# Attention with a convolved feed-forward layer on one core: probabilities cast and split by units of two slots, some squares halved on GpSimd, and a new order of all steps

## The chip, the core and the metric

The kernel runs on one core of a Trainium2 chip. That core has five engines with a queue of instructions each: TensorE (PE in the profile, with PEld for its weight loads), VectorE (DVE), ScalarE (ACT), GpSimd (POOL) and SyncE (SP), which here starts the DMA transfers. The metric is the device time of one execution in microseconds (us); lower is better.

## What is computed

The reference, cut to what matters. There are 8 batches and 12 heads, 448 positions, 64 features a head; the feed-forward layer goes from 768 to 1024 and back, with a convolution over 3 neighbouring positions as its gate.

```python
def _attn_ref(q, k, v, g_q, g_k):
    def rmsnorm(x, g):
        rms = np.sqrt(np.mean(x * x, axis=-1, keepdims=True) + 1e-06)
        return x / rms * g
    q_n, k_n = (rmsnorm(q, g_q), rmsnorm(k, g_k))
    scores = 1.0 / np.sqrt(q.shape[-1]) * np.matmul(q_n, k_n.transpose(0, 1, 3, 2))
    attn = np.exp(scores - np.max(scores, axis=-1, keepdims=True))
    attn = attn / (np.sum(attn, axis=-1, keepdims=True) + 1e-09)
    return np.matmul(attn, v).astype(np.float32)

def _moe_ref(x, w_in, conv_w, w_out):
    h = np.maximum(x @ w_in, 0.0)
    ...
    for k in range(K):
        conv_out += conv_w[k][None, None, :] * hp[:, k:k + S, :]
    gate = 1.0 / (1.0 + np.exp(-conv_out))
    return (h * gate @ w_out).astype(np.float32)
```

## The kernel before, in words

**Pairs and slots.** The work of attention goes by pairs of heads, 48 in all, six to a batch. The queries of a pair, 2 x 448 rows, are cut into seven blocks of 128 rows, which the code calls slots (`SLOTS`). The slots form four units (`GROUPS`): three units of two slots, one from each head, and a unit of one slot that holds the rest of both heads.

**Float32 by halves.** Most matmuls take numbers as two float16 parts: a cast ("hi") and the remainder of the cast ("lo"). Names ending in `_hi` and `_lo` make these parts.

**The steps of a pair.** `load_k` and `load_q` bring the rows (L355, L362). `square` makes the squares on ACT or POOL, `square_sum` adds them up by groups of 64 on DVE (L382), nine `rsqrt` steps make the factors for two pairs at once (a `duo`), and `apply_rms` applies them. `qk_transpose` turns q and k on PE (L481), `qk_hi` and `qk_lo` make their parts. `scores` multiplies a unit (L656), `soft_max` takes the maxima from PSUM on DVE (L664 when the two banks are neighbours, else L669), and `soft_exp` makes the exponentials of a slot on ACT (L679) into `e`, a ring of three buffers of one slot.

**Two ways to turn the probabilities.** Up to pair 9 PE transposes them (`p_transpose`, L726, and `p_evac`). From pair 10 on (`n1=10`, and `dg=7`: all seven slots) they are turned by DMA. `p_hi` casts a slot into `ph` (at the helper's line L83). `p_lo` subtracts the cast from the exponentials in two instructions, 384 and 64 columns (at L95). `p_turn` then transposes the whole unit by one DMA on SP (L717). `pv` (L815) multiplies with v, whose parts `v_hi` and `v_lo` (L792) make. `sum_add` to `sum_load` bring the sums of the exponentials to every partition by way of DRAM, with one small transpose on PE (L746), and `x_scale` (L822), `x_hi` and `x_lo` make x.

**Feed-forward.** For each batch `in_part` (L889) multiplies x by `w_in` in eight feature groups; relu, convolution, tanh and gate follow on ACT and DVE; `in_hi` and `in_lo` make the parts, `out_part` (L968) multiplies by `w_out`, `out_evac` and `out_store` write the result. Some feature groups of the first and last batch start early (`nf`, `nl`): their first matmuls run while later pairs of the batch are not done.

**The order.** No engine chooses at run time. The program writes down a plan: `at(time, step)` gives each step a due time, in which `base(n)` for pair n is `T0` us per pair for the first five pairs and `T` after that. `needs` lists what a step waits for, with the rings of buffers (`BUFS`) among it. `options` lists the engines a step may run on, with a cost for each. A list scheduler then takes, again and again, the step that can start soonest, with due times as a weight, and so fixes the engine, the PSUM bank and the place of every step in its engine's queue. Each queue is worked off strictly in that order. The constants in `PH` are the plan's parameters.

**Shared helpers.** `copy` (L83), `copy_scaled` (L87 to L89) and `binary` (L95) issue most casts and two-source operations; so one line of the profile stands for many steps, and the names of the tiles tell them apart.

Of the kernel before, what the change touches and what calls it, by code (L numbers as in the profile page):

```python
# [10 lines left out]
F32 = mybir.dt.float32  # L11
# [8 lines left out]
PH = dict(  # L20
    T0=11.354, N0=5, T=16.716, ti=26.404, si=4.968, so=8.683, hop=0.561, beta=0.03, wi0=-36.475,
    wi1=117.871, wo0=26.473, wo1=140.589, cw=-9.559, tg=-80.912, tl=42.69, ea=0.946, te=111.903,
    ep=0, hs=0, nf=2, adj=0.197, nz=8, ne=0, sc=5, tc=2, mc=8, p_qe=0.801, p_evac=0.876,
    p_hi=1.239, p_lo=6.052, p_rms=2.091, p_v=1.03, p_x=0.071, p_g=2.256, p_relu=0.553,
    p_cv=1.183, p_qz=0.843, p_ev=6.268, sp=0.158, nbulk=6, p_rs=0.05, p_sq=0.889, p_w=0.585,
    v0=-6.625, dg=7, n1=10, sw=0.0, nl=2, tj=0.0, pvs=1, pk=0.1, p_sa=0.167, p_ph=0.417,
    p_pl=0.839, nq=3, nk=95, p_qh=0.526, p_ql=0.365, tq=10.598, ti0=0.056, ti1=0.097, ti2=-0.224,
    ti3=0.742, ti4=-0.239, ti5=-0.006, ti6=0.553, ti7=-0.022, si0=0.995, si1=1.566, si2=1.683,
    si3=1.415, si4=1.633, si5=1.199, si6=1.05, si7=1.338, to0=0.019, to1=0.173, to2=-0.044,
    to3=0.041, to4=0.226, to5=-0.307, to6=-0.084, to7=0.325, so0=1.015, so1=1.613, so2=1.833,  # L30
    so3=1.736, so4=1.784, so5=1.547, so6=1.25, so7=1.038,
# [23 lines left out]
def tile_attention_moe(ctx: ExitStack, tc, q, k, v, g_q, g_k, w_in, conv_w, w_out, out):  # L55
# [41 lines left out]
    def move(e, dst, src):  # L97
# [9 lines left out]
        qkf=3, sq=2, st=2, qT=2, kT=2, qz=2, v=8, sst=6, e=3, PT=2, x=12, c=3,  # L107
# [24 lines left out]
    def bank(tag, key):  # L132
        i = bank_of[tag, key]
        assert bank_now[i] == (tag, key), f"{tag} {key} is gone"
        return banks[:, i]

    def old(tag, key):
        return rings[tag][tag, key]
# [20 lines left out]
    ebuf = [const.tile([P, 512], F32, name=f"e{i}") for i in range(BUFS["e"])]  # L159
# [216 lines left out]

    def square_sum(n):
        m = duo(n)[0]
        w = D // 2 if n < PH["hs"] else D
        if m == n:  # L380
            new("st", n, [P, 4, duo(n)[1], 2, 2 * NB], F32)
        nc.vector.tensor_reduce(  # L382
            old("st", m)[:, 0, n - m].rearrange("p i s -> p (i s)"),
            old("sq", n).rearrange("p i h t d -> p (i h t) d")[..., :w], axis=AX.X, op=ALU.add,
        )
# [144 lines left out]
    def plan_qk(n):  # L530
# [5 lines left out]
        if n < PH["hs"]:  # L536
            at(s - 23.0, square_half, n)
# [120 lines left out]
    def soft_max(n, g):  # L658
        js = GROUPS[g]
        st, at = new("sst", (n, g), [P, 2], F32), [bank_of["s", (n, j)] for j in js]  # L660
        for j in js:
            bank("s", (n, j))
        if at[-1] == at[0] + 1:
            nc.vector.tensor_reduce(  # L664
                st, banks[:, at[0] : at[0] + 2, :S], axis=AX.X, op=ALU.max, negate=True
            )
        else:
            for u, i in enumerate(at):
                nc.vector.tensor_reduce(  # L669
                    st[:, u : u + 1], banks[:, i, :S], axis=AX.X, op=ALU.max, negate=True  # L670
                )

    def soft_exp(n, j):
        if j == 0:
            new("rsum", n, [P, NS], F32)
        c = SLOTS[j]
        ring = rings.setdefault("e", Ring(BUFS["e"]))
        e = ring.put(("e", (n, j)), ebuf[ring.count % BUFS["e"]])
        nc.scalar.activation(  # L679
            e[:, :S], bank("s", (n, j))[:, :S], AF.Exp,  # L680
            bias=old("sst", (n, unit(j)[0]))[:, unit(j)[1] : unit(j)[1] + 1],
            accum_out=old("rsum", n)[:, c : c + 1],
        )


# [4 lines left out]
    def p_hi(n, j):  # L690
        u, i, _ = unit(j)
        if i == 0:
            ring = rings.setdefault("ph", Ring(BUFS["ph"]))
            ring.put(("ph", (n, u)), phbuf[ring.count % BUFS["ph"]])
        copy(
            on["p_hi", n, j], parts(n, j)[:, :4],
            old("e", (n, j)).rearrange("p (c k) -> p c k", c=4),
        )

    def parts(n, j):  # L700

        u, i, js = unit(j)
        m = len(js)
        blocks = old("ph", (n, u))[:, : 7 * m * P]
        return blocks.rearrange("p (c i k) -> p c i k", c=7, i=m)[:, :, i]

    def p_lo(n, j):
        p, e = parts(n, j), old("e", (n, j))[:, :S]
        binary(
            on["p_lo", n, j], p[:, 4:], e[:, : 3 * P].rearrange("p (c k) -> p c k", c=3),  # L710
            p[:, :3], ALU.subtract,
        )
        binary(on["p_lo", n, j], p[:, 3, 64:], e[:, 3 * P :], p[:, 3, :64], ALU.subtract)
# [8 lines left out]
    def p_transpose(n, j):  # L722
        ps, e = new_bank("t", ("p", n, j)), old("e", (n, j))
        for kt in range(NB):
            k0 = min(kt * P, S - P)
            nc.tensor.transpose(ps[:, kt * P : (kt + 1) * P], e[:, k0 : k0 + P], ident)  # L726
# [104 lines left out]
    def plan_attention(n):  # L831
# [3 lines left out]
        for j in range(NS):  # L835
            if unit(j)[1] == 0:
                at(s + j * d + 1.0, soft_max, n, unit(j)[0])
            at(s + j * d + 2.0, soft_exp, n, j)
            if j < nd(n):
                at(s + j * d + 3.0, p_hi, n, j)  # L840
                at(s + j * d + 4.0, p_lo, n, j)
                if j == unit(j)[2][-1]:
                    at(s + j * d + 5.0, p_turn, n, unit(j)[0])
                continue
            at(s + j * d + 4.0, p_transpose, n, j)
            at(s + j * d + 5.0, p_evac, n, j)
# [189 lines left out]
    def prepare():  # L1036
# [19 lines left out]
        for z in ebuf:  # L1056
            nc.gpsimd.memset(z[:, S:], 0.0)
# [48 lines left out]
    def needs(name, *a):  # L1106
# [109 lines left out]
        elif name == "v_load":  # L1216
            yield "pv", n - BUFS["v"], pvs(n - BUFS["v"])[-1]
# [30 lines left out]
        elif name == "soft_exp":  # L1248
# [3 lines left out]
            m, j = back(n, a[1], BUFS["e"])  # L1252
            yield ("p_lo" if j < nd(m) else "p_transpose"), m, j
            yield "sum_transpose", n - BUFS["rsum"]
        elif name == "p_hi":
            yield "soft_exp", *a
            if a[1] or not nd(n - 1):
                yield "p_hi", n, a[1] - 1
            else:
                yield "p_hi", n - 1, nd(n - 1) - 1  # L1260
            m, u = back(n, unit(a[1])[0], BUFS["ph"], NG)
# [4 lines left out]
        elif name == "p_turn":  # L1266
            for j in GROUPS[a[1]]:
                yield "p_lo", n, j
# [119 lines left out]
    def joined(n, g):  # L1388

        i, j = (bank_of["s", (n, j)] for j in (GROUPS[g][0], GROUPS[g][-1]))  # L1390
        return j == i + 1

    def options(name, *a):
        wo = a and a[0] == "out"
        dma = lambda kind, c, k=1, g="C": ("ACT" if kind in ON_ACT.split() else "SP", c, (g, k))
        dve, act, pool, pe = (lambda c, e=e: (e, c, None) for e in ("DVE", "ACT", "POOL", "PE"))
        return dict(
# [21 lines left out]
            square_sum=lambda: [dve(0.67 if a[0] < PH["hs"] else 1.21)],  # L1419
# [16 lines left out]
            soft_max=lambda: [dve(1.08 if joined(*a) else 0.61 * len(GROUPS[a[1]]))],  # L1436
# [34 lines left out]
            p_hi=lambda: [act(0.61), pool(0.62), dve(0.46)],  # L1471
            p_lo=lambda: [pool(1.22), dve(0.95)],
# [259 lines left out]
```

## Time and profile before

| what | value |
|---|---|
| median of 3 runs | 883.34 us (879.39 to 883.75) |
| the profiled execution | 882.48 us |
| its span, first to last instruction | 880.7 us |
| mean granted clock of TensorE | 0.984 |
| matmuls on PE | 5416 |
| DMA transfers | 132.69 MB, mean 151 GB/s |

How to read it. The page's first part gives each engine's busy time, its share of the span and its number of instructions. The second part cuts the span into 40 slices of 22 us, with a digit for tenths of busy time; `PEclk` is the TensorE clock that was granted, in tenths of full speed. The windows view gives the same for any stretch. In the lines view a row is a group of instructions of one line, engine, operation and tiles, with busy time, mean duration, and the idle time of the engine just before them. The waits view says who waited for whom: total, number of times, longest. The timeline lists instructions in order of time, with the idle time before one in brackets and what ended it.

### The profile page before, as it was taken

How to read it: one execution, taken by the hardware profiler on the slowest of the kernel's cores; microseconds unless marked ns; L12 is line 12 of the kernel's file. 1: busy time of each engine (PE TensorE's matmuls, PEld its weight loads, DVE VectorE, ACT ScalarE, POOL GpSimd, SP SyncE). 2: the span in 40 equal slices, each digit the busy share in tenths (PEclk: the TensorE clock that was granted, in tenths of full speed). 3: DMA queues.
4: the chain of work that ended last, by engine and by line, in shares of the span. 5: the costliest groups of instructions: out<-in, count | busy, mean ns of one | idle time of the engine just before them, and what ended most of it. 6: DMA issues, size and time to landing. Idle time of an engine off the chain costs nothing.

```text
span 880.7 us, 16865 instructions
## 1 busy us (share of the span) xinstructions
PE 817.6 (93%) x5416; PEld 417.4 (47%) x5416; DVE 732.5 (83%) x1256; ACT 685.1 (78%) x1571; POOL 642.0 (73%) x968
## 2 busy tenths in 40 slices
PE   1588999999998799999999999998999999999998
PEld 0343445545543345455444454454455554555554
DVE  6999999987899998999988887999899898972330
ACT  3677889888787978888887878897798878784441
POOL 4446667868787978988878987887787887884120
PEclk9989999999999899999999999999999999999999
DMA  8875542138997778897886898877796898458001
GB/s 248 216 225 130 162 108 67 44 83 185 175 191 147 159 168 179 168 188 163 180 184 134 183 173 184 184 163 153 176 183 147 165 191 163 102 93 163 28 13 60
DMA packets 344740, 132.69 MB, mean 151 GB/s; under 512 B 304612, under 2 KB 342860, under 8 KB 343884
## 3 DMA queue, kind: packets, MB, share of 16 engines
q1 hardware_dynamic: 344652, 131.62, 68.8%
q8 instruction: 43, 0.70, 0.3%
q14 instruction: 45, 0.37, 0.2%
HBM read 58.22 MB, written 11.18 MB: 79 GB/s over the span
## 4 chain that ended last, share of the span: by engine, by line
PE 64%; DVE 16%; DMA 6%; ACT 5%; POOL 4%; issue 4%; SPq 1%; DVEq 0%; ACTq 0%; POOLq 0%
PE banks L968 20%; PE banks L889 19%; PE banks L656 9%; PE banks L815 9%; PE banks L481 4%; PE banks L806 2%; POOL ph L95 2%; ACT e L679 2%; DMA wo<-in_moe_w_in_dram 2%; DMA rB<-rd 1%; PE banks L726 1%; DMA PT<-ph 1%; DVE st L382 1%; DVE wo L232 1%; DMA qk<-in_q_dram 1%
## 5 line engine op out<-in xcount | busy, mean ns | idle before, releaser
L95 POOL TENSOR_TENSOR ph<-e,ph 128x384 f16<-128x384 f32 x468 | 291.3, 647 | 53.1 <-ACT ph L83 49.5
L889 PE MATMUL banks<-x,wi 128*128 128x448 f16 x1152 | 250.1, 354 | 1.3 <-DVE kT L517 0.5
L968 PE MATMUL banks<-wo,gring 128*128 128x384 f16 (+1 forms) x1056 | 210.9, 328 | 2.1 <-DVE kT L517 1.8
L889 PEld LDWEIGHTS <-wi 128*128 128x128 f16 x1152 | 108.7, 98 | 102.0 <-issue 17.0
L83 ACT CAST ph<-e 128x512 f16<-128x512 f32 x244 | 147.7, 614 | 9.9 <-DMA PT<-ph 7.2
L968 PEld LDWEIGHTS <-gring 128*128 128x128 f16 (+1 forms) x1056 | 100.3, 99 | 78.1 <-issue 22.3
L656 PE MATMUL banks<-kT,qT 64*128 64x448 f16 x864 | 106.4, 361 | 8.8 <-DVE qT L519 6.3
L815 PE MATMUL banks<-PT,vp 128*64 128x448 f16 (+1 forms) x836 | 97.4, 363 | 4.5 <-ACT e L679 2.7
L95 POOL TENSOR_TENSOR sq<-qk,st 128x512 f32<-128x512 f32 (+1 forms) x78 | 85.4, 1108 | 6.2 <-DVE st L404 4.1
L481 PE MATMUL banks<-ident,sq 128*128 128x128 f32 (+1 forms) x364 | 60.8, 280 | 17.5 <-POOL sq L95 16.6
L95 POOL TENSOR_TENSOR x<-rB,x 128x448 f16<-128x448 f32 x48 | 51.5, 1073 | 23.5 <-ACT x L83 20.9
L815 PEld LDWEIGHTS <-vp 128*64 128x64 f16 (+1 forms) x836 | 41.8, 109 | 54.2 <-issue 33.8
L382 DVE TENSOR_REDUCE st<-sq 128x16 f32<-128x1024 f32 x48 | 57.6, 1206 | 9.6 <-ACT sq L369 9.6
L481 PEld LDWEIGHTS banks<-ident,sq 128*128 128x128 f32 (+1 forms) x364 | 44.5, 145 | 43.7 <-POOL sq L95 18.7
L656 PEld LDWEIGHTS <-qT 64*128 64x128 f16 x864 | 34.3, 95 | 64.2 <-issue 32.2
L726 PE MATMUL banks<-ident,e 128*128 128x128 f32 x280 | 45.8, 294 | 11.2 <-ACT PT L83 6.9
L822 DVE TENSOR_TENSOR rB<-banks,rB 128x448 f32<-128x448 f32 x48 | 29.6, 617 | 29.9 <-PE banks L815 14.5
L528 POOL COPY qz<-qT 64x128 f16<-64x128 f16 x89 | 32.9, 370 | 23.7 <-DVE qT L519 15.7
L726 PEld LDWEIGHTS banks<-ident,e 128*128 128x128 f32 x280 | 32.8, 147 | 31.4 <-ACT PT L83 13.3
L968 PE MATMUL banks<-wo,wi 128*128 128x384 f16 (+1 forms) x192 | 46.9, 326 | 0.0
L83 ACT COPY PT<-banks 128x512 f32<-128x512 f32 x66 | 38.0, 584 | 10.7 <-PE banks L726 10.2
L369 ACT ACTIVATE sq<-qk 128x1024 f32<-128x1024 f32 x35 | 36.7, 1050 | 7.8 <-DMA qk<-in_q_dram 7.8
(1154 smaller groups left out, 1726.9 us busy)
## 6 DMA issues: line engine op xcount, KB each, us to landing
qk<-in_q_dram SPq DMA_DIRECT2D x48, 224.0 KB
rB<-rd SPq DMA_DIRECT2D x96, 112.0 KB
qk<-in_k_dram SPq DMA_DIRECT2D x48, 128.0 KB
wo<-in_moe_w_in_dram SPq DMA_DIRECT2D x6, 1024.0 KB
v<-in_v_dram SPq DMA_DIRECT2D x48, 128.0 KB
gring<-in_moe_w_out_dram SPq DMA_DIRECT2D x8, 768.0 KB
qk<-in_k_dram SPq DMA_DIRECT2D x48, 96.0 KB
v<-in_v_dram SPq DMA_DIRECT2D x48, 96.0 KB
```

Source lines behind the costliest of these rows:

```text
L83: (nc.scalar.copy if e == "ACT" else elementwise(e).tensor_copy)(dst, src)
L95: elementwise(e).tensor_tensor(dst, a, b, op=op)
L369: nc.scalar.activation(sq, old("qkf", n), AF.Square)
L382: nc.vector.tensor_reduce(old("st", m)[:, 0, n - m].rearrange("p i s -> p (i s)"), old("sq", n).rearrange("p i h t d -> p (i h t) d")[..., ...
L481: nc.tensor.transpose(ps[:, t * w : t * w + m], x[:m, t], ident[:m, :m])
L528: e.tensor_copy(z[HALF[h], :, HALF[h]], old("qT", n)[HALF[h], :, t0 : t0 + 64])
L656: nc.tensor.matmul(ps[u][:, :S], lhs, kt[r, w], start=(i == 0), stop=(i == 2))
L726: nc.tensor.transpose(ps[:, kt * P : (kt + 1) * P], e[:, k0 : k0 + P], ident)
L815: nc.tensor.matmul(ps[HALF[h], :S], v[:m, w, h, c % 4], pt[:m, c, h * S : (h + 1) * S], start=(i == 0), stop=(i == len(PV7) - 1),)
L822: nc.vector.tensor_tensor(t, bank("m", ("v", n))[:, :S], t, op=ALU.mult)
L889: nc.tensor.matmul(ps[:, :S], wi[:, wl, c, fc * P : (fc + 1) * P], old("x", b * NP + c)[:, xl], start=(i == 0), stop=(i == 3 * NP - 1),)
L968: nc.tensor.matmul(ps[p0 : p0 + m, :NO2], g, wo[:, wl, fc, half * NO2 : (half + 1) * NO2], start=(i == 0), stop=(i == 3 * NFC - 1),)
```

## The change

1. `e` becomes a ring of two buffers, each with room for the two slots of a unit. `soft_exp` still makes one slot at a time and waits, at the first slot of a unit, for the remainders of the unit two before.
2. `p_hi` casts a unit in one instruction, through an access pattern that reads 4 x 128 columns of each slot at a stride of 448. `p_lo` makes the remainders of a unit in two instructions, 2 x 3 x 128 and 2 x 64 columns. `p_turn` waits for the one `p_lo`.
3. `square_half` existed, but ran for no pair (`hs=0`). A new `halved(n)` is true for `n >= 10` and `n % 4 < 2` (`hk=2`): there POOL adds the second half of each group of 64 squares to the first, and `square_sum` reduces 32 columns in place of 64.
4. The ring of v has 7 buffers in place of 8, and from the eighth load on a load waits for `v_lo` of the pair seven earlier, where that pair has one, in place of `pv` of the pair eight earlier.
5. The planner's costs for the new shapes are put in, and its parameters `PH` change: among others `T0` from 11.354 to 11.0, `T` from 16.716 to 16.382, `nl` from 2 to 3 and `nk` from 95 to 94. So the order of all steps, and the engine of some, is made anew.

The core of the diff:

```diff
-    T0=11.354, N0=5, T=16.716, ti=26.404, si=4.968, so=8.683, hop=0.561, beta=0.03, wi0=-36.475,
+    T0=11.0, N0=5, T=16.382, ti=26.404, si=4.968, so=8.766, hop=0.561, beta=0.03, wi0=-36.475,
...
-    v0=-6.625, dg=7, n1=10, sw=0.0, nl=2, tj=0.0, pvs=1, pk=0.1, p_sa=0.167, p_ph=0.417,
-    p_pl=0.839, nq=3, nk=95, p_qh=0.526, p_ql=0.365, tq=10.598, ti0=0.056, ti1=0.097, ti2=-0.224,
+    v0=-6.625, dg=7, n1=10, sw=0.0, nl=3, tj=-0.038, hk=2, pvs=1, pk=0.1, p_sa=0.167, p_ph=0.417,
+    p_pl=0.748, nq=3, nk=94, p_qh=0.526, p_ql=0.384, tq=10.598, ti0=0.04, ti1=0.123, ti2=-0.224,
...
-        qkf=3, sq=2, st=2, qT=2, kT=2, qz=2, v=8, sst=6, e=3, PT=2, x=12, c=3,
+        qkf=3, sq=2, st=2, qT=2, kT=2, qz=2, v=7, sst=6, e=2, PT=2, x=12, c=3,
...
-    ebuf = [const.tile([P, 512], F32, name=f"e{i}") for i in range(BUFS["e"])]
+    ebuf = [const.tile([P, 2 * S + 64], F32, name=f"e{i}") for i in range(BUFS["e"])]
...
+    def halved(n):
+
+        return n < PH["hs"] or n >= PH["n1"] and n % 4 < PH["hk"]
...
-        w = D // 2 if n < PH["hs"] else D
+        w = D // 2 if halved(n) else D
...
-        if n < PH["hs"]:
+        if halved(n):
             at(s - 23.0, square_half, n)
...
+    def e_slot(n, j):
+
+        u, i, _ = unit(j)
+        return old("e", (n, u))[:, S * i : S * (i + 1)]
...
+    def parts(n, u):
+
+        m, e = len(GROUPS[u]), old("e", (n, u))
+        blocks = old("ph", (n, u))[:, : 7 * m * P]
+        return (
+            blocks.rearrange("p (c i k) -> p i c k", c=7, i=m),
+            bass.AP(e.tensor, e.offset, [e.ap[0], [S, m], [P, 4], [1, P]]),
+        )
+
+    def p_hi(n, u):
+        ring = rings.setdefault("ph", Ring(BUFS["ph"]))
+        ring.put(("ph", (n, u)), phbuf[ring.count % BUFS["ph"]])
+        p, e = parts(n, u)
+        copy(on["p_hi", n, u], p[:, :, :4], e)
+
+    def p_lo(n, u):
+        p, e = parts(n, u)
+        w = on["p_lo", n, u]
+        binary(w, p[:, :, 4:], e[:, :, :3], p[:, :, :3], ALU.subtract)
+        binary(w, p[:, :, 3, 64:], e[:, :, 3, :64], p[:, :, 3, :64], ALU.subtract)
...
         elif name == "v_load":
-            yield "pv", n - BUFS["v"], pvs(n - BUFS["v"])[-1]
+            m = n - BUFS["v"]
+            yield ("v_lo", m) if nd(m) else ("pv", m, pvs(m)[-1])
...
-            m, j = back(n, a[1], BUFS["e"])
-            yield ("p_lo" if j < nd(m) else "p_transpose"), m, j
+            u, i, js = unit(a[1])
+            if i:
+                yield "soft_exp", n, a[1] - 1
+            m, u = back(n, u, BUFS["e"], NG)
+            if nd(m):
+                yield "p_lo", m, u
+            else:
+                for j in GROUPS[u]:
+                    yield "p_transpose", m, j
...
-            p_hi=lambda: [act(0.61), pool(0.62), dve(0.46)],
-            p_lo=lambda: [pool(1.22), dve(0.95)],
+            p_hi=lambda: [act(1.05 if m > 1 else 0.61), pool(1.1 if m > 1 else 0.62), dve(0.8 if m > 1 else 0.46)],
+            p_lo=lambda: [pool(2.08 if m > 1 else 1.22), dve(1.5 if m > 1 else 0.95)],
```

The helper that picks neighbouring PSUM banks for `soft_max` is written anew as `beside`; it issues the same instructions.

## What was predicted before the run

> **What bounds the kernel now.** I read the page's first two parts first, to see which engine is nearest to full and where it is not.
>
> ```profile
> span 880.7 us, 16865 instructions
> PE 817.6 (93%) x5416; PEld 417.4 (47%) x5416; DVE 732.5 (83%) x1256; ACT 685.1 (78%) x1571; POOL 642.0 (73%) x968
> PE   1588999999998799999999999998999999999998
> PEclk9989999999999899999999999999999999999999
> ```
>
> TensorE (PE) is nearest to full, and its row dips in two places: the first four slices, and the slices 12 and 13 (from 264 us on), where its granted clock dips too. So I asked the windows view for stretches cut at those places; the columns are length, then busy us of each engine, then clock, DMA share and GB/s.
>
> ```profile
> core 0: us, PE busy (x) PEld busy (x) DVE busy (x) ACT busy (x) POOL busy (x), PEclk, DMA share, GB/s
> 0.00:40.00 40.00, 14.14 (x75) 7.67 (x75) 31.39 (x57) 18.62 (x36) 16.21 (x43) 1.00 0.83 239
> 40.00:160.00 120.00, 106.16 (x629) 52.94 (x631) 115.57 (x189) 98.80 (x230) 82.74 (x85) 0.94 0.51 135
> 160.00:240.00 80.00, 79.91 (x528) 41.58 (x524) 69.86 (x126) 68.63 (x161) 62.85 (x90) 1.00 0.60 128
> 240.00:320.00 80.00, 68.60 (x471) 33.10 (x470) 74.84 (x122) 68.34 (x159) 66.97 (x106) 0.94 0.78 161
> 320.00:800.00 480.00, 471.65 (x3215) 238.59 (x3215) 423.11 (x737) 403.69 (x940) 400.55 (x634) 1.00 0.81 165
> 800.00:880.00 80.00, 77.19 (x503) 43.54 (x501) 17.74 (x28) 27.05 (x50) 12.69 (x14) 1.00 0.22 57
> ```
>
> Length less PE's busy time is PE's idle time: 25.9 and 13.8 us up to 160 us, where VectorE (DVE) is busy 115.57 of 120 us; 0.1 us to 240; 11.4 us from 240 to 320; 8.35 us in the next 480; 2.8 us at the end. After 160 us PE therefore sets the pace, and no other engine is full. What the change can win there is PE's idle time, 19.9 us without the end, and the clock that was not granted. More than half of that lies in one stretch, so I read the timeline there (start, length, engine, line, operation; the wait before it in brackets).
>
> ```profile
> 274.29 5.29 DVE L792 SCALAR_TENSOR_TENSOR vp<-v,vsc,vp 128x512 f16<-128x512 f32 x1
> 274.87 1.03 POOL L95 TENSOR_TENSOR x<-rB,x 128x448 f16<-128x448 f32 x1
> 275.86 1.04 POOL L95 TENSOR_TENSOR gring<-c_(1_3_2883,gring 128x448 f16<-128x448 f32 x1
> 276.85 1.18 POOL L95 TENSOR_TENSOR ph<-e,ph 128x384 f16<-128x384 f32 x2
> 277.98 1.05 POOL L95 TENSOR_TENSOR sq<-qk,st 112x512 f32<-112x512 f32 x1
> 279.50 1.14 DVE L669 TENSOR_REDUCE sst_(16_0_3032<-banks 128x1 f32<-128x448 f32 x2
> 281.82 0.27 PE L746 MATMUL banks<-ident,rsum 128*7 128x128 f32 x1 [3.98 <-DVE rsum L743]
> ```
>
> One DVE instruction with two SBUF tensor sources takes 5.29 us, while GpSimd (POOL) runs four steps without a gap; it ends 0.55 us after the last of them (279.03). The maximum of the next scores stands behind it on DVE, and PE stops for 3.98 us. The Trainium skill ("Advanced Engine Details and Errata", GPSIMD Details) says that Pool shares a read and a write interface with DVE and conflicts with DVE instructions that have two SBUF inputs; the timeline agrees, 5.29 us against a mean of 996 ns for that line.
>
> **The change, part by part.** The prices come from the lines view by shape (busy us, mean ns, idle before).
>
> ```profile
> L95 POOL TENSOR_TENSOR ph<-e,ph 128x384 f16<-128x384 f32 x234 | 223.7, 956 | 53.1 <-ACT ph L83 49.5 <-issue 0.5 <-POOL ph L95 0.3
> L83 ACT CAST ph<-e 128x512 f16<-128x512 f32 x244 | 147.7, 614 | 9.9 <-DMA PT<-ph 7.2
> L95 POOL TENSOR_TENSOR ph<-e,ph 128x64 f16<-128x64 f32 x234 | 79.0, 338 | 0.0
> L382 DVE TENSOR_REDUCE st<-sq 128x16 f32<-128x1024 f32 x48 | 57.6, 1206 | 9.6 <-ACT sq L369 9.6
> L792 DVE SCALAR_TENSOR_TENSOR vp<-v,vsc,vp 128x512 f16<-128x512 f32 x38 | 37.9, 996 | 0.1
> L578 DVE TENSOR_REDUCE vacc<-v 128x1 f32<-128x512 f32 x48 | 32.2, 674 | 1.4 <-DMA v<-in_v_dram 1.1
> L369 ACT ACTIVATE sq<-qk 128x1024 f32<-128x1024 f32 x35 | 36.7, 1050 | 7.8 <-DMA qk<-in_q_dram 7.8
> L95 POOL TENSOR_TENSOR sq<-qk,st 128x512 f32<-128x512 f32 x42 | 45.6, 1087 | 5.9 <-DVE st L404 4.1 <-DVE vsc L872 1.0
> L95 DVE TENSOR_TENSOR ph<-e,ph 128x384 f16<-128x384 f32 x32 | 23.8, 743 | 0.0
> L95 DVE TENSOR_TENSOR ph<-e,ph 128x64 f16<-128x64 f32 x32 | 18.0, 563 | 0.0
> ```
>
> *Casts by units.* Of each pair from 10 to 47 (38 pairs) six of the seven slots form three units of two, so 114 units; 244 of 266 casts are on ScalarE (ACT), so I count 105. Two casts of 614 ns become one of 128x1024, priced by the square of that shape, 1050 ns: 178 ns less each, 18.7 us off ACT.
>
> *Remainders by units.* From 64 to 384 elements POOL's time rises by 618 ns, 1.93 ns an element. A step of 768 is then 1698 ns and one of 128 is 462 ns: 2160 for what took 2 x (956 + 338) = 2588. With 234 of 266 slots on POOL that is 100 units at 0.43 us, 43 us off POOL. The other 14 units on DVE cost 2 x (743 + 563) ns now, mostly waiting; by the same line through its rows they would take 959 + 599, some 15 us less.
>
> *Halved squares.* `n % 4 < 2` from pair 10 picks 12, 13, 16, 17 and so on to 45: 18 pairs. Each adds a two-source step of 128x512 on POOL, 1087 ns, 19.6 us in all, and takes its sum on DVE from 1206 to about 674 ns, 9.6 us in all. The sum waits one step longer, but the plan puts it 22 us ahead of the pair's due time, which covers 1.1 us; without that cover each would cost its 0.55 us net.
>
> All this, 18.7 us of ACT, 23 of POOL and 25 of DVE, lies on engines that were idle 76, 79 and 57 us between 320 and 800 us. None of it is on PE's path by itself. It is worth what it takes out of PE's waits.
>
> *The stop between 240 and 320 us.* The order is made anew, so this queue of POOL steps need not stand beside that DVE step again, and POOL and DVE have less to do. If the stretch then idles at the rate of the 480 us behind it (8.35 / 480 x 80 = 1.4 us), 10.0 us go. Its clock of 0.94 over 80 us is 4.8 us not granted; PE was busy for 86% of it, so 4.1 us go as well. Sum 14.1 us. The Trainium skill ("TensorE: Matmul & The Clock Gate", Part 1) says that an idle window of about 3.4 us drops the clock to half until a busy one has passed; the 3.98 us wait beside a clock of 0.94 agrees, so stop and clock should go together.
>
> *Later release of the exponentials' buffer.* Three single slots become two units. An exponential that opens a unit still waits for the remainder of the third slot before it, except at the first slot of a pair, which now waits for the whole unit (4, 5). But that remainder ends later: behind a unit's last exponential come 1050 + 2160 ns where 614 + 956 + 338 stood, 1.30 us more. The waits view shows who waits now (us in total, times, longest).
>
> ```profile
> ACT e L679 <- DVE ph L95: 5.2, 3, 3.3
> ACT e L679 <- POOL ph L95: 4.4, 6, 1.2
> PE banks L815 <- ACT e L679: 2.7, 1, 2.7
> PE banks L968 <- ACT e L679: 0.8, 1, 0.8
> PE banks L656 <- ACT e L679: 0.7, 2, 0.5
> PEld L656 <- issue: 32.7, 85, 2.8
> PEld L815 <- issue: 33.8, 101, 2.0
> ```
>
> Nine waits, 9.6 us, become at most 9.6 + 9 x 1.30 = 21.3, a factor of 2.2. Behind such an exponential stand ACT's casts, copies out of PSUM and tanh steps, and PE waits for those. PE's idle time that ended with an exponential is 4.2 us; by that factor it grows by 5.0 us. At the other end the lighter ACT takes these 4.2 us away. I take +4, near the upper end, since the waits are there already.
>
> *At nothing.* p_turn keeps its 38 x 4 DMA transposes on SyncE and its last one per pair, which PV waits for, follows a single slot as before. The v ring of 7 lets a load go behind v_lo of the pair seven earlier instead of PV of the eighth: due about the same time, and seven pairs at T = 16.4 us cover the load. `nl=3` moves one more feature group of the last batch, 18 matmuls, ahead of a tail in which PE has no gap until its last matmul: the sum of PE's work stays. `nk=94` is still above the 48 pairs. What the new order does to the first 160 us I bound by DVE's idle time from 40 to 160, 4.4 us either way. Where PE changes between kinds of matmul its weight loads wait (66.5 us in 186 places, the two rows above); a tenth more or fewer such changes is 6.7 us at most. I take 0 for both, since no part of the change touches what they depend on.
>
> **Sum.** Profiled execution 882.48 (span 880.7 and 1.8 around it) - 14.1 + 4 = 872.4. The median of the runs, 883.34, lies 0.86 above the profiled one, so I forecast 873.
>
> **Rivals.** *A stop comes back elsewhere* (no measurable change). The new order knows the shared interface no better than the old one, and DVE keeps its 38 steps of L792. One stop of 14.1 us again: 873 + 14.1 = 887, or 883 if the units cost nothing. For it: smaller stops are strewn over the whole run, 8.35 us after 320. Against: POOL and DVE both do less.
>
> *The pace follows the new due times* (faster still). T and T0 bring pair 47's due time forward by 5 x 0.354 + 42 x 0.334 = 15.8 us. PE can follow only as far as it has idle time and clock to give: all 19.9 + 4.1 us gone would be 859. For it: less work on three engines. Against: the 8.35 us after 320 sit in small waits with many causes.
>
> *POOL's longer steps starve DVE* (slower). A step of 768 holds POOL 1.70 us where 384 held it 0.96. If each of the 38 L792 steps, and as many two-source steps again of the other lines, wait out the whole of one more such difference, DVE gets 76 x 0.74 = 56 us, as much as its 57 us of idle time between 320 and 800. From there DVE is full, as it is before 160 us. Then I expect two stops of the known size in place of one and the units' 4 us: 873 + 2 x 14.1 = 901 at worst, 890 to 895 when the second is small. For it: the 5.29 us. Against: POOL's steps become fewer and its queue shorter, and it was four steps in a row that did the harm, not one long one. The Trainium skill's sentence on the shared interface speaks for this rival.
>
> **How the numbers follow.** A measurement of this kernel can tell about 0.5%, 4.4 us. Forecast (865 to 879): 0.48. Pace (857 to 865): 0.15. Both are faster: 0.63. A stop comes back (879 to 888): 0.22. Starved DVE (888 to 901): 0.15. The range 858 to 890 takes in the forecast with its bounds for units, start and kinds of matmul, most of the pace and the beginning of the starved case, and leaves out some 0.15 to 0.2.
>
> **What would show it.** Right: POOL rows of 128x768 near 1.70 us and 128x128 near 0.46, about 100 of each; ACT casts of 128x1024 near 1.05 us; 18 reductions of 128x512 near 0.67 us on L382's successor; PE idle under 4 us and clock 1.00 in the 80 us around pairs 14 to 18; waits of ACT for `ph` at or under 21 us. Wrong: another PE gap over 3 us behind a DVE step of two sources; DVE above 95% busy after 320; PE busy time after 160 changed by more than 7 us, or the first exponential of pair 10 (188 us now) moved by more than 5 us (row below).
>
> ```profile
> 188.34 0.66 ACT L679 ACTIVATE e<-banks,sst_(10_0_1880 128x448 f32<-128x448 f32 x1
> ```

## The result

The changed kernel takes 891.49 us (median of 4 runs, 889.93 to 892.63) where the kernel before took 882.14 in the same comparison. The ratio is 1.0108, with a 95% interval of 1.0073 to 1.0143: slower by about 9.4 us, and outside the forecast range (873, 858 to 890).

The page of the changed kernel, first part and the two rows of the slices that were shown of before:

```profile
span 890.8 us, 16423 instructions
PE 817.2 (92%) x5416; PEld 418.7 (47%) x5416; DVE 718.7 (81%) x1214; ACT 681.3 (76%) x1476; POOL 630.2 (71%) x762
PE   0688899999998799999998999999999999999998
PEclk9978999999999899999999999999999999999999
```

PE does the same work in the same busy time (817.2 against 817.6 us). The other three engines are less busy than before, and the span is 10.1 us longer. So the 10 us are PE's idle time. PE's dip in slices 12 and 13 is still there. The windows view, with the same stretches as before:

```profile
0.00:40.00 40.00, 12.35 (x54) 6.70 (x55) 27.10 (x50) 16.98 (x33) 19.21 (x38) 1.00 0.86 253
40.00:160.00 120.00, 105.26 (x633) 52.96 (x631) 107.81 (x182) 99.01 (x230) 83.00 (x98) 0.93 0.48 128
160.00:240.00 80.00, 78.22 (x515) 41.32 (x513) 73.62 (x133) 69.49 (x151) 65.43 (x68) 1.00 0.57 118
240.00:320.00 80.00, 68.75 (x453) 32.16 (x453) 69.50 (x118) 64.80 (x141) 64.66 (x80) 0.91 0.88 167
320.00:800.00 480.00, 465.40 (x3203) 236.80 (x3198) 418.55 (x700) 397.75 (x860) 380.36 (x461) 1.00 0.83 164
```

Length less PE's busy time, before and after: 25.9 and 27.6 up to 40 us, 13.8 and 14.7 to 160, 0.1 and 1.8 to 240, 11.4 and 11.2 to 320, 8.4 and 14.6 to 800. The stretch that was to win 10 us wins 0.2, and its clock falls from 0.94 to 0.91. The biggest loss, 6.2 us, lies in the 480 us after it, where the forecast had put nothing.

The stop of before has a successor at the same place. The timeline of the changed kernel:

```profile
279.02 3.51 DVE L541 COPY qz<-qT 64x128 f16<-64x128 f16 x1
279.32 1.03 POOL L95 TENSOR_TENSOR gring<-c_(1_3_2864,gring 128x448 f16<-128x448 f32 x1
280.31 1.03 POOL L95 TENSOR_TENSOR sq<-qk,st 112x512 f32<-112x512 f32 x1
281.31 1.17 POOL L95 TENSOR_TENSOR ph<-e,ph 128x384 f16<-128x384 f32 x2
283.50 0.37 PE L751 MATMUL banks<-ident,rsum 128*7 128x128 f32 x1 [2.58 <-DVE rsum L748]
```

This time it is a float16 copy on VectorE that takes 3.51 us; a copy of the same shape took 0.19 us at 280.67 us of the kernel before. It ends 0.05 us after a queue of GpSimd steps, and PE waits 2.58 us behind it.

The new shapes in the lines view (busy us, mean ns, idle before):

```profile
L95 POOL TENSOR_TENSOR ph<-e,ph 128x768 f16<-128x768 f32 x103 | 171.5, 1665 | 56.9 <-ACT ph L83 37.7 <-issue 14.9 <-POOL qz L541 1.0
L83 ACT CAST ph<-e 128x1024 f16<-128x1024 f32 x107 | 111.4, 1041 | 6.8 <-DMA PT<-ph 5.0
L95 POOL TENSOR_TENSOR ph<-e,ph 128x128 f16<-128x128 f32 x103 | 45.7, 444 | 0.0
L378 ACT ACTIVATE sq<-qk 128x1024 f32<-128x1024 f32 x39 | 41.0, 1052 | 8.8 <-DMA qk<-in_q_dram 8.8
L95 POOL TENSOR_TENSOR sq<-sq 128x512 f32<-128x512 f32 x18 | 22.9, 1271 | 3.0 <-ACT sq L378 1.8 <-POOL qz L541 0.6 <-POOL ph L95 0.5
L95 DVE TENSOR_TENSOR ph<-e,ph 128x128 f16<-128x128 f32 x11 | 17.9, 1627 | 0.0
L95 DVE TENSOR_TENSOR ph<-e,ph 128x768 f16<-128x768 f32 x11 | 13.1, 1188 | 0.0
L395 DVE TENSOR_REDUCE st<-sq 128x16 f32<-128x512 f32 x18 | 12.2, 677 | 0.7 <-POOL sq L95 0.7
```

The change does what it says, at nearly the forecast prices: 1665 and 444 ns on POOL for 1698 and 462, 1041 on ACT for 1050, 677 on DVE for 674. Two are off. The added halves take 1271 ns for 1087, and the 11 units that stayed on DVE take 1188 + 1627 ns where 959 + 599 was forecast: a step of 128 columns is the longer of the two, so most of its time is probably waiting.

### The profile page after: what moved, and what is told of

The parts are those of the page before. It is cut to its first block, busy times and chain, and to the rows that moved or that the text cites. A ratio compares the mean times of both kernels' runs of the same rounds, so it can differ in the third digit from the quotient of the medians.

```text
span 890.8 us, 16423 instructions
## 1 busy us (share of the span) xinstructions
PE 817.2 (92%) x5416; PEld 418.7 (47%) x5416; DVE 718.7 (81%) x1214; ACT 681.3 (76%) x1476; POOL 630.2 (71%) x762
## 4 chain that ended last, share of the span: by engine, by line
PE 63%; DVE 15%; ACT 6%; DMA 5%; issue 5%; POOL 4%; SPq 1%; ACTq 0%; DVEq 0%; POOLq 0%
PE banks L973 19%; PE banks L894 17%; PE banks L669 9%; PE banks L820 7%; PE banks L811 4%; PE banks L494 3%; PE banks L731 3%; DMA PT<-ph 2%; ACT e L684 2%; DMA rB<-rd 2%; DVE ph L95 1%; POOL sq L95 1%; DMA qk<-in_q_dram 1%; DVE qz L541 1%; ACT ph L83 1%
## 5 line engine op out<-in xcount | busy, mean ns | idle before, releaser
L95 POOL TENSOR_TENSOR ph<-e,ph 128x768 f16<-128x768 f32 (+3 forms) x276 | 255.0, 945 | 57.8 <-ACT ph L83 38.4
L894 PE MATMUL banks<-x,wi 128*128 128x448 f16 x1152 | 253.9, 354 | 1.3 <-ACT c_('o'_0_2_1_2783 L87 0.7
L973 PE MATMUL banks<-wo,gring 128*128 128x384 f16 (+1 forms) x1056 | 210.7, 327 | 1.9 <-DVE rB L827 1.2
L894 PEld LDWEIGHTS <-wi 128*128 128x128 f16 x1152 | 108.6, 98 | 101.2 <-issue 18.1
L83 ACT CAST ph<-e 128x1024 f16<-128x1024 f32 (+1 forms) x144 | 134.0, 931 | 9.1 <-DMA PT<-ph 7.0
L973 PEld LDWEIGHTS <-gring 128*128 128x128 f16 (+1 forms) x1056 | 100.0, 99 | 74.5 <-issue 17.5
L95 POOL TENSOR_TENSOR sq<-qk,st 128x512 f32<-128x512 f32 (+1 forms) x89 | 99.0, 1127 | 12.9 <-DVE st L417 6.6
L494 PE MATMUL banks<-ident,sq 128*128 128x128 f32 (+1 forms) x364 | 61.1, 281 | 23.1 <-POOL sq L95 18.4
L395 DVE TENSOR_REDUCE st<-sq 128x16 f32<-128x1024 f32 (+1 forms) x48 | 48.3, 1007 | 10.9 <-ACT sq L378 9.7
L731 PE MATMUL banks<-ident,e 128*128 128x128 f32 x280 | 44.5, 293 | 10.2 <-ACT PT L83 5.5
L378 ACT ACTIVATE sq<-qk 128x1024 f32<-128x1024 f32 x39 | 41.0, 1052 | 8.8 <-DMA qk<-in_q_dram 8.8
L973 PE MATMUL banks<-wo,wi 128*128 128x384 f16 (+1 forms) x192 | 46.9, 326 | 0.0
L83 ACT CAST x<-rB 128x448 f16<-128x448 f32 x39 | 22.0, 563 | 29.7 <-DVE rB L827 29.2
L541 POOL COPY qz<-qT 64x128 f16<-64x128 f16 x81 | 29.1, 359 | 21.3 <-DVE qT L532 17.4
```

The costliest lines, as they stand in the source:

```text
L83: (nc.scalar.copy if e == "ACT" else elementwise(e).tensor_copy)(dst, src)
L95: elementwise(e).tensor_tensor(dst, a, b, op=op)
L378: nc.scalar.activation(sq, old("qkf", n), AF.Square)
L395: nc.vector.tensor_reduce(old("st", m)[:, 0, n - m].rearrange("p i s -> p (i s)"), old("sq", n).rearrange("p i h t d -> p (i h t) d")[..., ...
L494: nc.tensor.transpose(ps[:, t * w : t * w + m], x[:m, t], ident[:m, :m])
L541: e.tensor_copy(z[HALF[h], :, HALF[h]], old("qT", n)[HALF[h], :, t0 : t0 + 64])
```

## The experiments

I began with two theories. *Holds*: a longer GpSimd step keeps the interface that it shares with VectorE, VectorE falls behind, and PE stops. This is the prediction's slower rival. *Order*: the parts do little, and the new order of all steps happens to be worse. After e3 came a third, *halves*: the added GpSimd steps cost more than the shorter sums win. After e8 came a fourth, for the stretch from 240 to 320 us alone, *filler*: PE has run out of feed-forward matmuls there.

Ratios below are to the kernel before, with 95% intervals, timed side by side. "At a fixed order" means that the planner's order, engines and banks were kept and only the instructions of some steps changed.

**e1: the shared interface by itself.** The loop of a kernel that otherwise only writes zeros:

```python
for count, width in ((4, 384), (10, 384), (2, 768), (5, 768)):
    for kind in ("two", "psum", "copy16", "sum"):
        nc.vector.memset(src[:, :1], 0.0)
        nc.gpsimd.tensor_tensor(flag[:, :64], src[:, :64], hi[:, :64], op=ALU.subtract)
        for i in range(count):
            nc.gpsimd.tensor_tensor(lo[i % 4][:, :width], src[:, :width], hi[:, :width], op=ALU.subtract)
        nc.vector.tensor_reduce(a[:, :1], flag[:, :2], AX.X, ALU.max)
        dve(kind)
        nc.vector.tensor_reduce(b[:, :1], lo[(count - 1) % 4][:, :2], AX.X, ALU.max)
```

> This kernel leaves the whole computation out and writes zeros. It lets GpSimd run streaks of two-source steps without a gap (4 or 10 of 128x384, 2 or 5 of 128x768), and starts one VectorE step of 512 columns behind the first of them: two SBUF sources, one source in PSUM, a float16 copy, or a sum. Theory 'holds' (one GpSimd step keeps the shared interface until it ends, and VectorE gets in only between steps or behind the streak): the two-source step and the copy take their own 0.2 to 0.7 us plus up to 0.9 us beside steps of 384 and up to 1.65 us beside steps of 768, or the whole rest of the streak, 3 to 8 us; the PSUM and the sum steps stay near 0.65 us. Theory 'order' (the shared interface matters little, the new order has its stops from elsewhere): all four kinds stay within 0.3 us of their time without a streak, whatever the width.

Measured, in the timeline of this kernel: a streak of steps of 384 and one of steps of 768, with the two-source step on DVE in each, and the step whose first source is in PSUM beside 768.

```profile
26.12 9.16 POOL L58 TENSOR_TENSOR lo<-src,hi 128x384 f16<-128x384 f32 x10
26.38 1.19 DVE L45 TENSOR_TENSOR res<-a,b 128x512 f32<-128x512 f32 x1
...
79.55 8.46 POOL L58 TENSOR_TENSOR lo<-src,hi 128x768 f16<-128x768 f32 x5
79.81 1.92 DVE L45 TENSOR_TENSOR res<-a,b 128x512 f32<-128x512 f32 x1
...
88.70 0.68 DVE L47 TENSOR_TENSOR res<-bank,b 128x512 f32<-128x512 f32 x1
```

The two-source step takes 1.19 us beside steps of 384 and 1.92 beside steps of 768. It gets in when the running GpSimd step ends, not behind the streak (9.16 and 8.46 us). The float16 copy behaves alike, 0.91 and 1.64 us. The step with a source in PSUM and the sum take 0.68 and 0.69 us beside either. So the hold is real, and a step of 768 makes it 0.73 us longer, against 0.74 in the prediction. It is the sharing that the Trainium skill states ("Advanced Engine Details and Errata", GPSIMD Details) with its size. What e1 does not show is the 5.29 us of the profile before, where a DVE step waited through seven GpSimd steps.

**e2: units at the old order.** Casts and remainders by units, at the place of the unit's last slot in the order of before; four exponentials move back by 2 to 5 places, because two buffers of a unit demand it. The small ring `mx` also goes from 10 buffers to 6, which no theory is about.

```diff
...
-        copy(
-            on["p_hi", n, j], parts(n, j)[:, :4],
-            old("e", (n, j)).rearrange("p (c k) -> p c k", c=4),
-        )
...
+        u = last_of("p_hi", n, j)
+        if u is None:
+            return
...
+        p, e = parts(n, u)
+        copy(on["p_hi", n, j], p[:, :, :4], e)
```

> The kernel before with its own order, engines and banks; only the casts and remainders go by units (at the place of the unit's last slot), with a ring of two buffers for the exponentials, for which four exponentials move back by 2 to 5 places. Theory 'holds': slower than before by 3 to 10 us, 885 to 892, with more VectorE steps stretched by over 1 us than the 10 of before (20 to 30). Theory 'order': 868 to 882, since POOL and ACT only get lighter.

Measured: 886.01 us, ratio 1.0047 (1.0018 to 1.0075), some 4 us slower. The waits view shows where (in this kernel the exponential is line 681):

```profile
ACT e L681 <- POOL ph L96: 15.2, 13, 2.4
ACT e L681 <- DVE ph L96: 4.5, 2, 3.0
PE banks L832 <- ACT e L681: 2.8, 2, 2.6
PE banks L657 <- ACT e L681: 2.2, 4, 1.1
PE banks L482 <- ACT e L681: 1.3, 3, 0.7
PE banks L985 <- ACT e L681: 1.2, 1, 1.2
```

ACT's waits for the buffer went from 9.6 to 19.7 us, and PE's idle time that ended with an exponential from 4.2 to 7.5 (without that of the transposes before pair 10, 1.1 and 0.8). This is the later release, as the prediction had it: at most 21.3, and +4. That it makes up the 4 us is not shown: of the 4.6 us that PE idles more in the profiled execution, 3.6 lie before 160 us, where no cast by units runs yet.

Both theories had a number for e2 and *order*'s is out. *Holds* also forecast more stretched VectorE steps. I count a step as stretched when it takes over 1 us more than the lower quartile of its operation, shape and tiles in all 19 runs of whole kernels: 13 before, 21 in e2 and 28 in the changed kernel (the expectations count 10 and 28). So e2 does not tell the buffer from the shared interface.

**e3: halves too, at the old order.** As e2, with `square_half(n)` right ahead of the sum of the 18 pairs.

> As e2, and GpSimd also adds the halves of the squares of the 18 pairs, right ahead of their sums. Theory 'holds': within 4 us of e2, since steps of 512 on POOL are no longer than others that it has; slower than before. Theory 'order': 866 to 882.

Measured: 898.12 us, ratio 1.0198 (1.0168 to 1.0227), 12 us above e2. Neither theory had that; e3 has 25 stretched steps. The adds stand in POOL's queue where no plan had made room, so this bounds their price from above.

**e4: remainders slot by slot again, at the new order.**

```diff
-        binary(w, p[:, :, 4:], e[:, :, :3], p[:, :, :3], ALU.subtract)
-        binary(w, p[:, :, 3, 64:], e[:, :, 3, :64], p[:, :, 3, :64], ALU.subtract)
+        for i in range(len(GROUPS[u])):
+            binary(w, p[:, i, 4:], e[:, i, :3], p[:, i, :3], ALU.subtract)
+            binary(w, p[:, i, 3, 64:], e[:, i, 3, :64], p[:, i, 3, :64], ALU.subtract)
```

> The changed kernel with its own order, engines and banks; only each unit's remainders are issued slot by slot again (384 and 64 columns, four instructions in place of two), so that GpSimd has some 37 us more to do. Theory 'holds': faster than the changed kernel, 878 to 887, with fewer VectorE steps stretched by over 1 us (10 to 18 where the changed kernel has 28). Theory 'order': 891 to 898, the same stops and a busier GpSimd.

Measured: 895.35 us, ratio 1.0155 (1.0115 to 1.0194). The stretched steps fall from 28 to 16, as *holds* had it, but the time does not follow: no gain, where *holds* had 878 to 887 us. GpSimd has more to do in e4, so this alone does not settle it. But e8 below is as slow as the changed kernel with 10 stretched steps, so they are not needed for such a loss, and e16 is as fast as before with 22, so they are not enough for it. *Holds* falls as the main cause; that some of the loss is its own is not ruled out.

**e5 and e12: no halves, new orders.** `hk=0`, and in e12 `T=16.4` besides.

> The changed kernel without the halved squares (hk=0), its order planned anew from the same parameters. Theory 'halves' (the 18 added GpSimd steps cost more than VectorE wins by them): 878 to 886. Theory 'order' (what a new order happens to bring outweighs the parts): anything from 880 to 900, no side more likely. Theory 'holds' (the remainders' steps of 768 cost): within 3 us of the changed kernel, 888 to 895.

> The changed kernel without the halves, T from 16.382 to 16.4: a second order for the units alone. Theory 'halves': below the changed kernel again, 878 to 888. Theory 'order' alone: 880 to 900, as likely above the changed kernel as below.

Measured: e5 883.43 us, ratio 1.0027 (0.9999 to 1.0055), as *halves* had it, within *order*'s range too, and out of *holds*'s. e12 887.91 us, 1.0107 (1.0058 to 1.0155), no better than the changed kernel. Two orders that differ by a thousandth in T lie 0.8% apart, so e5 alone proved nothing about the halves.

**e6, e8, e11: the kernel before in other orders.** e6 has the changed kernel's `PH` and none of its parts. e8 and e11 only move T, from 16.716 to 16.7 and to 16.73.

> The kernel before with the changed kernel's parameters of the plan and nothing else: casts and remainders by slots, no halves, so the order alone is made anew. Theory 'order': slower than before, 885 to 898. Theories 'holds' and 'halves': as before, 878 to 886.

> The kernel before with one parameter of the plan moved by a thousandth (T from 16.716 to 16.7), which means nothing but makes another order. Theory 'order': it differs from before by 4 us or more, to either side, more likely slower. Theories 'holds' and 'halves': as before within 3 us, since the work is the same to the instruction.

> The kernel before with one parameter of the plan moved by a thousandth the other way (T from 16.716 to 16.73): a second order that means nothing. Theory 'order': 884 to 895, again slower than before, which then has a better order than its neighbours. Theory 'halves': 878 to 885.

Measured: e6 885.70 us, 1.0059 (1.0026 to 1.0093), which lies in the ranges of both sides; e8 890.07 us, 1.0104 (1.0071 to 1.0137); e11 887.64 us, 1.0088 (1.006 to 1.0117). All three are slower than before, with the same work. e8 alone loses as much as the whole change, and at the same place: its PE idles 15.4 us from 320 to 800, where before idles 8.4 and the changed kernel 14.6. Not every order loses there: e12 idles 7.9 us after 320, but 61.1 before it, where before idles 51.2.

**e7: both parts, the parameters of before.**

> The changed kernel with both of its parts (units, halves), planned with the parameters of before. Theories 'holds' and 'halves': slower than before, as the changed kernel is, 887 to 896. Theory 'order': anything from 880 to 905; it would differ from the changed kernel by more than 4 us.

Measured: 893.88 us, 1.0150 (1.0103 to 1.0198); it lies above the changed kernel, but the intervals overlap. *Order* had it apart from the changed kernel by more than 4 us, which is not shown; the range of the other two, 887 to 896, holds it.

**e9 and e10: half of the halves, at the new order.** e9 takes the adds out and keeps the short sums, e10 the reverse.

> The changed kernel in its own order, with the 18 GpSimd adds of halves taken out and the sums still over 32 columns: it leaves half of the squares of those 18 pairs out of their norm. It shows what VectorE's shorter sums are worth when GpSimd does not pay for them. Theory 'halves' (the added GpSimd steps are the loss): 879 to 886. Theory 'order': 888 to 894, as the changed kernel, since the places of all other steps are the same.

> The changed kernel in its own order, with the adds of halves kept and the sums of those pairs over all 64 columns again (so that their second halves are counted twice). It has GpSimd's cost without VectorE's gain. Theory 'halves': 889 to 896, close to the changed kernel, because the shorter sums win little. Theory 'order': the same to 4 us slower, 890 to 896.

Measured: e9 884.95 us, 1.0061 (1.0042 to 1.0081); e10 888.56 us, 1.0102 (1.0058 to 1.0145). Without the adds some 4 us go, as *halves* had it, though the intervals of e9 and the changed kernel just overlap. Without the short sums nothing is lost that can be measured (both theories had e10 a little slower): 9.6 us of VectorE's time show no worth on PE's path.

**e17 and e18: no halves at all, at a fixed order.** e17 in the order of the changed kernel, e18 in that of e16 (below).

```diff
-        sq = old("sq", n)
-        binary("POOL", sq[..., : D // 2], sq[..., : D // 2], sq[..., D // 2 :], ALU.add)
+        return
...
-        w = D // 2 if halved(n) else D
+        w = D
```

> The changed kernel in its own order, every other step at its place, with neither the adds of halves nor the shorter sums. Theory 'halves' (they cost by themselves): 1.002 to 1.007 of before, 4 us or more under the changed kernel's 1.0108. Theory 'order' (the halves are paid for by the shorter sums; where the steps stand decides): 1.008 to 1.014.

> The same for e16's order (so0=2.4), which was as fast as before with the halves in it. Theory 'halves': 0.993 to 0.996 of before, faster than both. Theory 'order': 0.997 to 1.003, no change from e16.

Measured: e17 886.46 us, 1.0059 (1.0035 to 1.0084), the same as e9. e18 882.53 us, 1.0009 (0.9992 to 1.0026), not faster than e16 with the halves. *Halves* is met by e17 and missed by e18, *order* the other way round. So the halves probably cost about 0.5% in the slow order (the intervals just overlap) and nothing in the fast one.

**e13 to e16: feed-forward work moved to the stretch from 240 to 320 us.** One parameter, `so0`, puts the output matmuls of the first batch later: in the kernel before 2.5 (e13) and 1.4 (e14), in the changed kernel without halves 2.4 (e15), in the changed kernel 2.4 (e16).

> The kernel before with one parameter of the plan changed, so0 from 1.015 to 2.5, which puts the output matmuls of the first batch later, so that the plan has 22 us of feed-forward matmuls between the scores of pairs 16 and 19 where before has 12. Theory 'filler' (PE idles between 240 and 320 us because it has run out of feed-forward matmuls there): idle time there under 7 us (before 11.4) at a clock of 0.97 or more; the whole time 4 to 8 us under that of the other new orders of before, 878 to 884. Theory 'holds' (the idle time there comes from VectorE steps that GpSimd keeps waiting): idle time there stays at 10 to 13 us, the whole at 884 to 892.

> As e13 with so0=1.4: 24 us of feed-forward matmuls between the scores of pairs 16 and 19, most of them at pair 17. Theory 'filler': idle time from 240 to 320 us under 8 us, the whole 878 to 885. Theory 'holds': 10 to 13 us, the whole 884 to 892.

> The changed kernel without the halves, so0 from 1.431 to 2.4: 22 us of feed-forward matmuls between the scores of pairs 16 and 19 (20 in e5). Theory 'filler': little changes from e5, idle time from 240 to 320 us 9 to 11 us, the whole 878 to 886. Theory 'halves': below the changed kernel in any case, under 888.

> The changed kernel with so0 from 1.431 to 2.4: 20 us of feed-forward matmuls between the scores of pairs 16 and 19 where the changed kernel has 15. Theory 'filler': idle time from 240 to 320 us 7 to 10 us (changed kernel 11.2), clock above 0.93, the whole 885 to 890. Theory 'holds': no change there, 888 to 895.

What suggested it were the windows of the feed-forward matmuls alone, in the kernel before, `in_part` (L889) and then `out_part` (L968):

```profile
280.00:320.00 40.00, 3.21 (x9) 0.87 0.69 143
360.00:800.00 440.00, 144.04 (x651) 1.00 0.80 163
...
280.00:320.00 40.00, 9.30 (x96) 0.87 0.69 143
360.00:800.00 440.00, 156.32 (x907) 1.00 0.80 163
```

From 280 to 320 us PE has 12.5 us of them, from 360 on 27 us in every 40. The idea was that without them PE waits out each wait of the attention steps. The same two windows in the changed kernel (L894, L973), and then in e16:

```profile
280.00:320.00 40.00, 8.01 (x32) 0.83 0.78 146
280.00:320.00 40.00, 5.31 (x56) 0.83 0.78 146
```

```profile
280.00:320.00 40.00, 7.58 (x33) 1.00 0.92 174
280.00:320.00 40.00, 14.94 (x128) 1.00 0.92 174
```

With 22.5 us of filler in place of 13.3 the clock is 1.00 in place of 0.83. The larger stretches of e16:

```profile
160.00:240.00 80.00, 73.22 (x473) 38.33 (x470) 70.21 (x127) 67.06 (x149) 64.69 (x70) 0.98 0.53 111
240.00:320.00 80.00, 74.79 (x538) 36.73 (x536) 71.01 (x132) 68.41 (x150) 69.65 (x80) 1.00 0.89 178
320.00:800.00 480.00, 473.61 (x3231) 240.15 (x3228) 417.77 (x708) 401.47 (x873) 380.53 (x457) 1.00 0.83 168
```

PE idles 5.2 us from 240 to 320, where the changed kernel idled 11.2, and 6.8 from 160 to 240, where it idled 1.8. Most of that idle time has moved ahead: 12.0 us for 13.0 in the two stretches together. The fuller clock shows little in time, since PE's whole busy time is 816.5 us for 817.2. Most of e16's gain, 8.2 of 12.2 us of span, stands behind 320: 6.4 us idle for 14.6. In all e16 takes 879.96 us, ratio 0.9990 (0.996 to 1.002): the whole change, with one number of the plan altered, is as fast as the kernel before, and no version that was run is measurably faster. e15: 881.65 us, 0.9997 (0.9974 to 1.002), idle 7.7 us from 240 to 320. e14: 882.77 us, 1.0029 (0.9998 to 1.0059), 6.8 us. e13 is the miss: it has 19.5 us of filler from 280 to 320, and idles 12.1 us from 240 to 320 all the same; 894.11 us, 1.0139 (1.0095 to 1.0183), with 15.0 us idle after 320. *Filler* has e14 in its ranges. In e15 and e16 the idle time fell, and below its ranges (9 to 11 and 7 to 10 us); e16's whole time lies below its range too (885 to 890).

The traces suggest why e13 missed. Here is the longest stretched VectorE step from 270 to 320 us beside the feed-forward work that ran from 280 to 320 and PE's idle time, all in us:

| run | feed-forward | longest stretched step | idle 240 to 320 | idle 160 to 320 |
|---|---|---|---|---|
| before | 12.5 | 5.29 | 11.4 | 11.5 |
| the change | 13.3 | 3.51 | 11.2 | 13.0 |
| e5 | 16.6 | 4.86 | 11.7 | 14.2 |
| e8 | 10.7 | none | 11.2 | 12.2 |
| e13 | 19.5 | 4.86 | 12.1 | 15.5 |
| e14 | 19.5 | 2.20 | 6.8 | 9.5 |
| e15 | 21.2 | 2.23 | 7.7 | 14.1 |
| e16 | 22.5 | 1.75 | 5.2 | 12.0 |
| e17 | 12.2 | 3.36 | 10.7 | 13.2 |
| e18 | 22.5 | 1.75 | 5.2 | 11.7 |

The stretch idles little only where it has much feed-forward work and no long stretched step. e8 idles with no stretched step at all, and e13 with much feed-forward work. The last column says what that was worth. Against the same kernel without the shift (e14 against before, e15 against e5, e16 against the change, e18 against e17) the two stretches together idle only 0.1 to 2.0 us less: the idle time mostly went to the 80 us before.

All orders together, as ratios to the kernel before:

| what the kernel does | orders planned anew | at a fixed order |
|---|---|---|
| the work of before | 1.0029, 1.0059, 1.0088, 1.0104, 1.0139 | 1 (before) |
| units alone | 0.9997, 1.0027, 1.0107 | 1.0047 (e2); 1.0059 (e17); 1.0009 (e18) |
| units and halves | 0.9990, 1.0108 (the change), 1.0150 | 1.0198 (e3) |

The three rows of new orders overlap almost fully; their means are 1.0084, 1.0044 and 1.0083. What this kernel takes is set by where the steps fall more than by these parts.

## Why the prediction was wrong, point by point

- **What bounds the kernel** was right: PE's idle time after 160 us is all that the parts can win, and the result is an increase of PE's idle time at unchanged busy time, most of it after 160 us.
- **The prices** were right to 4%, but for the halves (1271 ns, not 1087) and the units on DVE. **The sums of work taken off** were not: ACT's busy time fell by 3.8 us, not 18.7, POOL's by 11.8, not 23, DVE's by 13.8, not 25. The new plan moved other steps to the engines that had become free: ACT makes 39 squares where it made 35, and VectorE 15 of the copies into `qz`, 16.3 us, where it made 7 in 4.0.
- **The stop, -14.1 us: this is the step that failed first.** I took one DVE step of 5.29 us for the cause of the idle time from 240 to 320 us, and a new order for its cure. (Four GpSimd steps were counted beside it; the timeline has seven that overlap it.) The stretch idles 11.2 us in the changed kernel, its clock is 0.91, and a copy held for 3.51 us stands at the same place. Nor is the held step the whole cause: e8 has none in the stretch and idles 11.2 us too. The stretch idles 10.2 to 17.4 us in every run but e14, e15, e16 and e18, which have both much feed-forward work and no long held step there, and even these give most of it back before 240 us. The windows of L889 and L968 would have shown the lack of feed-forward work before the run, though not that more of it would hardly shorten the whole. For the 4.1 us of clock in the sum there is no sign either: the clock of the stretch went from 0.94 to 0.91, and PE's busy time stayed.
- **The new order at 0 us: this failed too, and is the larger error of principle.** "No part of the change touches what they depend on" is true of the work and not of the order. Five orders of the unchanged work took 0.3 to 1.4% more, 7.4 us on the mean; before is the best of its neighbours. The bounds that I gave, 4.4 us for the first 160 us and 6.7 for PE's weight loads, left out the 480 us where most of the loss fell (14.6 us idle, not 8.4).
- **The later release, +4 us**, was right in mechanism at the old order (e2): ACT's waits doubled. That e2 as a whole is also some 4 us slower may be luck, since most of the added idle time of its profile lies before 160 us. In the new order the planner had gone round it: the waits of ACT for `ph` are 6.2 us there.
- **The rivals.** The result lies in the band of "POOL's longer steps starve DVE" (0.15). Its price of 0.74 us for one longer hold was right (e1), and stretched steps did become more, 28 for 13, but they are not the main cause: they fell to 16 in e4 without a gain, e8 loses as much with 10, and e16 loses nothing with 22. That the time landed in this band is luck. VectorE was not full after 320 us either (418.6 of 480 us). "A stop comes back" had the right idea of an order that knows no better, and of a held step that returns; the price it gave is that of one stop, and most of the loss lies elsewhere.
- **The signs.** The prices and numbers of the new rows came as listed, and none of the signs of being wrong did: no PE gap over 3 us behind such a DVE step (2.58 and 2.95 us were the longest after 160 us), the first exponential of pair 10 at 191.19 us for 188.34, PE's busy time after 160 us 2.3 us longer. Only the sign for the stretch itself, idle under 4 us at a clock of 1.00, failed. Signs that look at single places missed a loss that is strewn over the whole run.
- **Still open:** which waits make the 6 us more after 320 us, since no single one there is over 2 us. Of PE's listed waits there 9.8 us end with a VectorE step, 5.8 in the kernel before, but also 13.7 in e8, which has none of the parts. Open too are whether the halves cost by themselves outside the one order where they seem to; and why a DVE step sometimes waits through many GpSimd steps, when e1 lets it in after one.

## What to carry to other kernels

Where a list scheduler makes the whole order anew, a change cannot be judged by one run against a chosen order: first time a few orders of the unchanged work (here they spread over 1.4%), and keep the order fixed to price a part; even then the price holds for that order (the halves cost about 0.5% in one and nothing in the other). Before a stop of the bounding engine is put down to the wait that ended it, count what other work that engine had at that point, and look at the sum over neighbouring stretches: moving the filler here moved the idle time and hardly shortened it. Work taken off engines that do not bound the kernel showed no gain here; do not count on one until a wait that PE feels is named.

## What the runs showed of the hardware

In e1 a DVE step with two SBUF sources, or a float16 copy in SBUF, that starts while GpSimd works on a two-source step waits until that step ends: 1.19 and 0.91 us beside 128x384, 1.92 and 1.64 us beside 128x768. A step with one source in PSUM or a sum shows no such wait (0.68 and 0.69 us beside either). GpSimd pays as well: its streak of ten steps of 384 takes 9.16 us beside the two-source step and 8.71 beside the PSUM one.

```profile
35.84 8.71 POOL L58 TENSOR_TENSOR lo<-src,hi 128x384 f16<-128x384 f32 x10
45.25 0.91 DVE L49 COPY resh<-h 128x512 f16<-128x512 f16 x1
97.27 1.64 DVE L49 COPY resh<-h 128x512 f16<-128x512 f16 x1
106.00 0.69 DVE L51 TENSOR_REDUCE res<-a 128x1 f32<-128x512 f32 x1
```
